# Attention value product with the softmax weights stationary, and v with a column of ones moving

## The chip, the cores and the metric

The program runs on one core of a Trainium2 chip. The metric is the device time of one execution in microseconds (us). Most executions of one kernel agree within 0.3%; lowest and highest are given beside each median. Where two kernels are compared, the ratio is the mean time of one kernel's fast runs over the mean of the other's fast runs of the same rounds on the same chip; it is therefore not quite the ratio of the medians that are quoted beside it.

Engines: PE is TensorE's matmul, PEld its weight load, DVE is VectorE, ACT is ScalarE, POOL is GpSimd, SP is SyncE. The argument takes it that each engine works through its instructions in the program's order, and that only weight loads run ahead.

## The reference, cut to what matters

Block-sparse attention (batch 4, 8 heads, 768 tokens, head dimension 64), then two matmuls that are multiplied, then two more matmuls.

```python
scores = (1 / sqrt(64)) * q @ k^T            # per batch and head
scores = where(mask, scores, -1e9)           # 32x32 blocks; mask is the same for all heads
attn = exp(scores - max) / sum(exp(scores - max))
x = (attn @ v) with heads side by side       # 3072 tokens x 512
out = ((x @ w1) * (x @ w2)) @ w3 @ w_out     # 512 -> 1024 -> 1024 -> 512
```

Both kernels fold `w3 @ w_out` once (the "fold"), and use that as one matrix. Both skip the maximum and multiply the exponentials by a 0/1 mask.

## The kernel before

Work goes in 72 rounds. A round is one (batch b, block of 256 queries t, half of the heads Q, third of the keys kp). Three rounds with kp = 0, 1, 2 make one accumulation. PE's order in a round is: scores of this round, value product of the round before, then two pieces of "filler" (the fold, later the FFN), which run while ACT and DVE turn scores into weights.

```python
def scores(b, t, Q, kp, i):                  # twice a round, i = 0, 1
    ... 4 matmuls into s (PSUM, 2 banks, pool ps_s of two such tiles)
    nc.scalar.activation(e, s, AF.Exp, scale=1.0 / 8.0)
    nc.vector.tensor_tensor(e, e, mask[...], op=ALU.mult)

def values(b, t, Q, kp):
    ...
    for k2 in range(2):
        for part in range(3):                # v columns 0-31, 32-63, then ones
            for g in range(4):               # four heads, one 32-row strip of PSUM each
                rhs = es[i][:, h, k2 * QT:(k2 + 1) * QT]          # 256 queries moving
                ... matmul(d[rows, :], lhsT=ones, rhs=rhs)        # part 2: denominators
                ... matmul(o[rows, ...], lhsT=vn[...32 columns], rhs=rhs)

def normalize(b, t, Q):                      # after kp = 2
    nc.scalar.activation(ln, d, AF.Ln)
    nc.scalar.activation(rec, ln, AF.Exp, scale=-1.0)
    nc.vector.tensor_tensor(X[i][...], o, rec, op=ALU.mult)       # x stands turned already

# FFN filler: ps_f is a pool of two PSUM banks, shared by pa, pb and po
pa: 4 matmuls of 512 columns -> nc.scalar.copy(a, p)
pb: 4 matmuls of 512 columns -> nc.vector.tensor_tensor(hT[:, f, :], p, a, op=ALU.mult)
po: 8 matmuls of 512 columns -> copy -> output DMA

for s, g in enumerate(groups):               # cuts marked ...
    scores(b, t, Q, kp, 0)
    scores(b, t, Q, kp, 1)
    if prev is not None:
        values(*prev)
        finish(prev)                         # normalize if kp == 2
    ...
    pop(0 if s < 3 else 2)                   # two pieces of filler
    prev = g
```

Inputs are loaded and cast by DMAs that GpSimd issues, all in one queue: q, k, v of the first four heads of batch 0, then `w_out` and `w3` with the other four heads in between, then `w1`, `w2`, with later batches behind them.

The softmax here doesn't subtract the row's maximum and nothing guards it: scores larger than these inputs give would overflow.

Of the kernel before, what the change touches and what calls it, by code (L numbers as in the profile page):

```python
# [8 lines left out]
F32 = mybir.dt.float32  # L9
BF16 = mybir.dt.bfloat16  # L10
I32 = mybir.dt.int32
AF = mybir.ActivationFunctionType
ALU = mybir.AluOpType
# [4 lines left out]
def kernel(  # L18
# [16 lines left out]
    nc = tc.nc  # L35
    B, H, S, D = q.shape
    BLK = 32
    NB = S // BLK
    C = S // 128
# [3 lines left out]
    QT = 256  # L43
    NT = S // QT

    def pool(name, bufs, **kw):
        return ctx.enter_context(tc.tile_pool(name=name, bufs=bufs, **kw))

    const = pool("const", 1)
    wts = pool("wts", 1)  # L50
    nat = pool("nat", 4)
    natv = pool("natv", 8)
    qkt = pool("qkt", 8)
    epool = pool("epool", 6)
    small = pool("small", 2)
# [5 lines left out]
    ps_o = pool("ps_o", 1, space=PSUM)  # L61
    ps_f = pool("ps_f", 2, space=PSUM)
# [13 lines left out]
    qn, kn, vn = {}, {}, {}  # L76
# [16 lines left out]
    wf_sb = wts.tile([128, NF, d_model], BF16, tag="wf")  # L93

    def load_w12(ap, t):
        src = ap.rearrange("(Q g s d) f -> g d Q s f", Q=2, g=4, s=2)
        for g in range(4):
            for Q in range(2):
                nc.gpsimd.dma_start(out=t[32 * g:32 * g + 32, 2 * Q:2 * Q + 2, :], in_=src[g][:, Q])


    load_pair(0, 0, "qk")
# [25 lines left out]
    load_pair(0, 3)  # L128
    load_w3(4, NF)
    load_w12(moe_w1, w1_sb)  # L130
    load_w12(moe_w2, w2_sb)

    ident = const.tile([128, 128], BF16, tag="ident")
    nc.vector.tensor_scalar(ident, in0=idf, scalar1=0.0, scalar2=None, op0=ALU.is_equal)
    ones = const.tile([128, 32], BF16, tag="ones")
    nc.vector.memset(ones, 1.0)
    hot = const.tile([NB, C, 128], BF16, tag="hot")
    hot_hi = const.tile([NB, C, 128], BF16, tag="hot_hi")
    nc.vector.tensor_scalar(hot, in0=hotf, scalar1=0.0, scalar2=None, op0=ALU.is_ge)
# [14 lines left out]
    for r in range(3):  # L154
# [3 lines left out]
                                op=ALU.is_equal)  # L158
# [12 lines left out]
    def build_mask(t):  # L171
        for kp in range(3):
            mp = ps_f.tile([128, 512], F32, tag="f", name="mp")
            for k2 in range(2):
                nc.tensor.matmul(mp[:, k2 * QT:(k2 + 1) * QT], lhsT=hot[:, 2 * kp + k2, :],
                                 rhs=G[:, t * QT:(t + 1) * QT], start=True, stop=True)
            nc.scalar.copy(mask[:, t, kp, :], mp)  # L177


    QK = {}  # L180

    def transposes(b, pr):
        tp = ps_s.tile([128, 2, 1024], BF16, tag="s", name="tp")
        for x, src in ((0, qn[b, pr]), (1, kn[b, pr])):
            for c in range(C):
                for h in range(2):
                    nc.tensor.transpose(tp[64 * h:64 * h + 64, x, c * 128:(c + 1) * 128],  # L187
                                        src[:, h, c, :], ident)
        t = qkt.tile([128, 2, S], BF16, tag="qkt", name="qkt")
        nc.vector.tensor_copy(t, tp[:, :, :S])  # L190
        QK[b, pr] = t

    E = {}

# [16 lines left out]
    acc = {}  # L211

    def values(b, t, Q, kp):
        if kp == 0:
            acc["o"] = ps_o.tile([128, 512], F32, tag="o", name="o")
            acc["d"] = ps_o.tile([128, QT], F32, tag="d", name="d")
        o, d = acc["o"], acc["d"]
        es = [E.pop((b, t, Q, kp, i)) for i in range(2)]
        for k2 in range(2):
            kc = 2 * kp + k2  # L220
            first, last = kc == 0, kc == C - 1
            for part in range(3):
                for g in range(4):
                    i, h = divmod(g, 2)
                    rhs = es[i][:, h, k2 * QT:(k2 + 1) * QT]
                    rows = slice(32 * g, 32 * g + 32)
                    if part == 2:
                        nc.tensor.matmul(d[rows, :], lhsT=ones, rhs=rhs, start=first, stop=last,  # L228
                                         skip_group_check=True)
                    else:  # L230
                        nc.tensor.matmul(o[rows, part * QT:(part + 1) * QT],  # L231
                                         lhsT=vn[b, 2 * Q + i][:, h, kc, 32 * part:32 * part + 32],
                                         rhs=rhs, start=first and part == 0, stop=last,
                                         skip_group_check=True)

    X = {}

    def normalize(b, t, Q):
        o, d = acc["o"], acc["d"]
        i, half = divmod(b * NT + t, 2)  # L240
        if i not in X:
            X[i] = xpool.tile([128, 4, 512], BF16, tag="x", name="x")
        ln = small.tile([128, QT], F32, tag="ln", name="ln")
        nc.scalar.activation(ln, d, AF.Ln)  # L244
        rec = small.tile([128, 1, QT], F32, tag="rec", name="rec")
        nc.scalar.activation(rec[:, 0, :], ln, AF.Exp, scale=-1.0)  # L246
        nc.vector.tensor_tensor(  # L247
            X[i][:, 2 * Q:2 * Q + 2, half * QT:(half + 1) * QT],
            o.rearrange("p (s n) -> p s n", s=2),
            rec.to_broadcast((128, 2, QT)), op=ALU.mult)  # L250


    fill = deque()
# [27 lines left out]
    def ffn(i):  # L281
        x = X[i]
        hT = hpool.tile([128, NF, 512], BF16, tag="h", name="h")
        box = {}

        def pa(f):
            def go():
                p = ps_f.tile([128, 512], F32, tag="f", name="pa")
                for c in range(4):
                    nc.tensor.matmul(p, lhsT=w1_sb[:, c, f * 128:(f + 1) * 128], rhs=x[:, c, :],  # L290
                                     start=c == 0, stop=c == 3)
                a = apool.tile([128, 512], BF16, tag="a", name="a")
                nc.scalar.copy(a, p)  # L293
                box["a"] = a
            return go

        def pb(f):
            def go():
                p = ps_f.tile([128, 512], F32, tag="f", name="pb")
                for c in range(4):  # L300
                    nc.tensor.matmul(p, lhsT=w2_sb[:, c, f * 128:(f + 1) * 128], rhs=x[:, c, :],  # L301
                                     start=c == 0, stop=c == 3)
                nc.vector.tensor_tensor(hT[:, f, :], p, box["a"], op=ALU.mult)  # L303
            return go

        def po(n, half):
            def go():
                if half == 0:
                    box["o"] = ps_f.tile([128, 512], F32, tag="f", name="po")
                for f in range(4 * half, 4 * half + 4):  # L310
                    nc.tensor.matmul(box["o"], lhsT=hT[:, f, n * 128:(n + 1) * 128],  # L311
                                     rhs=wf_sb[:, f, :], start=f == 0, stop=f == NF - 1)
                if half == 1:
                    b, c = divmod(4 * i + n, C)
                    ob = opool.tile([128, 512], F32, tag="ob", name="ob")
                    nc.vector.tensor_copy(ob, box["o"])  # L316
                    nc.sync.dma_start(out=outv[b, c], in_=ob)
            return go

        for f in range(NF):  # L320
            fill.append(pa(f))
            fill.append(pb(f))
        for n in range(4):
            fill.append(po(n, 0))
            fill.append(po(n, 1))


    transposes(0, 0)
    transposes(0, 1)
    for t in range(NT):  # L330
        build_mask(t)

# [11 lines left out]
    done = {}  # L344
    n_ffn = 0
    prev = None

    def finish(g):
        nonlocal n_ffn
        b, t, Q, kp = g  # L350
        if kp == 2:
            normalize(b, t, Q)
            done[b * NT + t] = done.get(b * NT + t, 0) + 1
            while done.get(2 * n_ffn) == 2 and done.get(2 * n_ffn + 1) == 2:
                ffn(n_ffn)
                n_ffn += 1

    def pop(n):
        for _ in range(n):
            if fill:  # L360
                fill.popleft()()

    for s, g in enumerate(groups):
        b, t, Q, kp = g
        r = s % 18
        scores(b, t, Q, kp, 0)
        scores(b, t, Q, kp, 1)
        if prev is not None:
            values(*prev)
            finish(prev)  # L370
        if b + 1 < B and r in (2, 5, 8, 11):
            load_pair(b + 1, (r - 2) // 3)
        if b == 0 and s in (7, 8):
            transposes(0, s - 5)
        elif b + 1 < B and r in (12, 13, 15, 16):
            transposes(b + 1, (12, 13, 15, 16).index(r))
        pop(0 if s < 3 else 2)
        prev = g
    values(*prev)
    finish(prev)  # L380
    while fill:
        pop(1)
    order.__exit__(None, None, None)
# [30 lines left out]
```

## Time and profile before

299.68 us, median of 2 runs (299.67 to 299.69).

| what | view | value |
|---|---|---|
| busy share PE / DVE / ACT | the page's first part | 91% / 65% / 63% |
| PE in the chain that ended last | the chain of waits | 68% |
| a round with FFN filler: scores / values / filler | the timeline | 0.54 / 0.77 / 1.83 us |
| three such rounds | the timeline | 9.62 us |
| first value matmul | the timeline | 23.70 us |

The first part of the page of the kernel before. Columns: engine, busy us, share of the span, instructions.

```profile
PE 272.0 (91%) x3412; PEld 141.2 (47%) x3412; DVE 194.2 (65%) x308; ACT 189.5 (63%) x250; POOL 49.6 (17%) x81
```

One round of the kernel before, from the timeline of PE. Columns: start, length to the end of the last matmul, engine, source line, what is written from what, shape, count. Lengths overlap, because matmuls are pipelined; so read costs as differences of starts.

```profile
136.77 0.61 PE L201 MATMUL s<-qkt 64*128 64x256 bf16 x8
137.31 0.40 PE L231 MATMUL o<-e,vn 128*32 128x256 bf16 x8
137.54 0.28 PE L228 MATMUL d<-e,ones 128*32 128x256 bf16 x4
137.65 0.39 PE L231 MATMUL o<-e,vn 128*32 128x256 bf16 x8
137.87 0.28 PE L228 MATMUL d<-e,ones 128*32 128x256 bf16 x4
138.08 1.04 PE L290 MATMUL pa<-x,w_sb 128*128 128x512 bf16 x4
138.96 1.03 PE L301 MATMUL pb<-x,w_sb 128*128 128x512 bf16 x4
139.92 0.28 PE L201 MATMUL s<-qkt 64*128 64x256 bf16 x2
```

Scores take 137.31 - 136.77 = 0.54 us, the value product 138.08 - 137.31 = 0.77, pa and pb 1.84. There is no gap: PE is the limit here. Four value matmuls of 256 columns run side by side on 32-column strips, 0.11 us per four.

In the waits of PE (columns: who waited for whom, us in total, times, longest) in the kernel before:

```profile
PE o L231 <- DVE x L247: 1.8, 2, 1.1
```

The trace has the fold's transposes, eight in a row with a full weight load each.

```profile
48.69 0.62 PE L259 MATMUL w3p<-ident,w_sb 128*128 128x128 bf16 x8
```

One of them lasts 0.22 us, so the other seven started within 0.40 us, 57 ns apart: a 128x128 weight load is hidden behind 128 moving columns.

### The profile page before, as it was taken

The numbers are of one execution on the slowest core, as the hardware profiler recorded it, in microseconds if no ns is written. First come the engines' busy times: TensorE is split into PE (matmuls) and PEld (weight loads), VectorE is DVE, ScalarE is ACT, GpSimd is POOL, SyncE is SP. The second block draws the span as 40 slices with busy tenths as digits, with TensorE's granted clock in tenths as the row PEclk, the third lists the DMA queues.
The fourth block names the chain that finished last, engine by engine and source line by source line (L and its number), as shares of the span: only waits on it lengthen the run. The fifth ranks groups of instructions, "written<-read, shape, count | busy, mean of one in ns | idle before, by whom it ended". The sixth has DMA issues, their size and how long they took to land.

```text
span 298.6 us, 7850 instructions
## 1 busy us (share of the span) xinstructions
PE 272.0 (91%) x3412; PEld 141.2 (47%) x3412; DVE 194.2 (65%) x308; ACT 189.5 (63%) x250; POOL 49.6 (17%) x81
## 2 busy tenths in 40 slices
PE   0479888987999999999999999999999999999994
PEld 0335455555454455555455455555445445444441
DVE  3616787778767776776777677677767676643332
ACT  1088766656688886576867887657988778721310
POOL 8634487222200000332100000000000000000000
PEclk9999999999999999999999999999999999999998
DMA  7999999973420002757311000011000120003003
GB/s 96 150 204 207 206 173 186 180 106 55 66 44 2 0 2 108 131 69 106 55 37 73 35 2 2 2 72 70 3 2 1 52 93 2 0 2 140 0 12 129
DMA packets 20053, 21.46 MB, mean 72 GB/s; under 512 B 1588, under 2 KB 14900, under 8 KB 20020
## 3 DMA queue, kind: packets, MB, share of 16 engines
q0 software_dynamic: 16528, 14.68, 32.5%
q1 hardware_dynamic: 3492, 6.29, 5.6%
q8 instruction: 26, 0.43, 0.6%
q14 instruction: 7, 0.06, 0.1%
HBM read 29.36 MB, written 6.29 MB: 119 GB/s over the span
## 4 chain that ended last, share of the span: by engine, by line
PE 68%; ACT 15%; DVE 10%; issue 4%; POOL 1%; ACTq 0%; POOLq 0%
PE o L231 13%; PE pa L290 12%; PE pb L301 12%; ACT e L206 10%; PE po L311 10%; PE s L201 9%; PE wp L272 5%; DVE x L247 4%; PE d L228 4%; ACT rec L246 3%; PE tp L187 3%; DVE qkt L190 2%; ACT ln L244 2%; DVE e L207 1%; ACT mask L177 1%
## 5 line engine op out<-in xcount | busy, mean ns | idle before, releaser
L206 ACT ACTIVATE e<-s 128x1024 bf16<-128x1024 f32 x144 | 139.5, 1021 | 54.8 <-PE s L201 54.4
L207 DVE TENSOR_TENSOR e<-e,mask 128x1024 bf16<-128x1024 bf16 x144 | 99.1, 691 | 55.3 <-ACT e L206 55.3
L231 PE MATMUL o<-e,vn 128*32 128x256 bf16 x1152 | 54.8, 278 | 3.8 <-DVE x L247 1.8
L201 PE MATMUL s<-qkt 64*128 64x256 bf16 x576 | 47.5, 277 | 5.6 <-DVE qkt L190 3.9
L290 PE MATMUL pa<-x,w_sb 128*128 128x512 bf16 x192 | 49.7, 381 | 0.0
L301 PE MATMUL pb<-x,w_sb 128*128 128x512 bf16 x192 | 49.2, 379 | 0.0
L303 DVE TENSOR_TENSOR h<-pb,a 128x512 bf16<-128x512 f32 x48 | 33.1, 690 | 21.2 <-PE pb L301 21.2
L311 PE MATMUL po<-wf_sb,h 128*128 128x512 bf16 x192 | 44.5, 380 | 0.0
L293 ACT CAST a<-pa 128x512 bf16<-128x512 f32 x48 | 28.0, 583 | 26.1 <-PE pa L290 25.7
L228 PE MATMUL d<-e,ones 128*32 128x256 bf16 x576 | 42.4, 276 | 0.0
L201 PEld LDWEIGHTS <-qkt 64*128 64x128 bf16 x576 | 22.8, 95 | 37.5 <-issue 34.8
L231 PEld LDWEIGHTS <-vn 128*32 128x32 bf16 x1152 | 26.9, 96 | 20.5 <-issue 18.4
L301 PEld LDWEIGHTS <-w_sb 128*128 128x128 bf16 x192 | 18.7, 98 | 24.1 <-issue 2.6
L311 PEld LDWEIGHTS <-h 128*128 128x128 bf16 x192 | 17.5, 98 | 21.9 <-issue 2.7
L290 PEld LDWEIGHTS <-w_sb 128*128 128x128 bf16 x192 | 15.7, 98 | 21.1 <-issue 7.0
L316 DVE COPY ob<-po 128x512 f32<-128x512 f32 x24 | 16.5, 688 | 10.2 <-PE po L311 10.2
L85 POOL DMA_DIRECT2D qn<-in_q_dram x16 | 11.7, 728 | 66.7 <-PE tp L187 59.4
L247 DVE TENSOR_TENSOR x<-o,rec 128x512 bf16<-128x512 f32 x24 | 16.6, 692 | 1.6 <-ACT rec L246 0.9
L228 PEld LDWEIGHTS <-ones 128*32 128x32 bf16 x576 | 17.0, 98 | 0.4
L190 DVE COPY qkt<-tp 128x1536 bf16<-128x1536 bf16 x16 | 15.2, 950 | 1.3 <-PE tp L187 1.3
L272 PE MATMUL wp<-wo_sb,w3t_sb 128*128 128x512 bf16 x64 | 15.2, 380 | 0.0
L85 POOL DMA_DIRECT2D vn<-in_v_dram x16 | 11.6, 726 | 17.5 <-PE d L228 14.6
(54 smaller groups left out, 125.7 us busy)
## 6 DMA issues: line engine op xcount, KB each, us to landing
out_dram<-ob SPq DMA_DIRECT2D x24, 256.0 KB, 2.0
qn<-in_q_dram POOLq DMA_DIRECT2D x16, 192.0 KB, 4.2
kn<-in_k_dram POOLq DMA_DIRECT2D x16, 192.0 KB, 4.8
vn<-in_v_dram POOLq DMA_DIRECT2D x16, 192.0 KB, 5.8
w_sb<-in_moe_w_dram POOLq DMA_DIRECT2D x8, 256.0 KB, 10.6
w_sb<-in_moe_w_dram POOLq DMA_DIRECT2D x16, 128.0 KB, 5.3
wo_sb<-in_moe_w_out_dram POOLq DMA_DIRECT2D x1, 1024.0 KB, 11.3
rand_sb<-in_sampled_blocks_dram SPq DMA_DIRECT2D x1, 0.6 KB
```

Source lines behind the costliest of these rows:

```text
L201: nc.tensor.matmul(s[:, h, k2 * QT:(k2 + 1) * QT], lhsT=qk[64 * h:64 * h + 64, 1, kc * 128:(kc + 1) * 128], rhs=qk[64 * h:64 * h + 64, 0, ...
L206: nc.scalar.activation(e, s, AF.Exp, scale=1.0 / 8.0)
L207: nc.vector.tensor_tensor(e, e, mask[:, t, kp:kp + 1, :].to_broadcast((128, 2, 512)), op=ALU.mult)
L228: nc.tensor.matmul(d[rows, :], lhsT=ones, rhs=rhs, start=first, stop=last, skip_group_check=True)
L231: nc.tensor.matmul(o[rows, part * QT:(part + 1) * QT], lhsT=vn[b, 2 * Q + i][:, h, kc, 32 * part:32 * part + 32], rhs=rhs, start=first and ...
L247: nc.vector.tensor_tensor(X[i][:, 2 * Q:2 * Q + 2, half * QT:(half + 1) * QT], o.rearrange("p (s n) -> p s n", s=2), rec.to_broadcast((128 ...
L272: nc.tensor.matmul(box["p"], lhsT=w3t_sb[:, j, i * 128:(i + 1) * 128], rhs=wo_sb[:, j, :], start=j == 0, stop=j == NF - 1)
L290: nc.tensor.matmul(p, lhsT=w1_sb[:, c, f * 128:(f + 1) * 128], rhs=x[:, c, :], start=c == 0, stop=c == 3)
L293: nc.scalar.copy(a, p)
L301: nc.tensor.matmul(p, lhsT=w2_sb[:, c, f * 128:(f + 1) * 128], rhs=x[:, c, :], start=c == 0, stop=c == 3)
L303: nc.vector.tensor_tensor(hT[:, f, :], p, box["a"], op=ALU.mult)
L311: nc.tensor.matmul(box["o"], lhsT=hT[:, f, n * 128:(n + 1) * 128], rhs=wf_sb[:, f, :], start=f == 0, stop=f == NF - 1)
```

## The change

Its intent: swap the operands of the value product. The weights `e` (128 keys x 128 queries) are loaded, and v with a column of ones (65 columns) moves. One matmul then gives 64 outputs and the denominator; 24 matmuls of 256 columns (four abreast) become 16 of 65 columns. The price is that x comes out with tokens on partitions: it is divided there (ln and exp on ACT disappear), and then turned by four PE transposes with a copy from PSUM. v has to be widened to 65 columns, which GpSimd does.

```diff
-    natv = pool("natv", 8)
+    natv = pool("natv", 4)
+    vpool = pool("vpool", 8)
@@ loads of w1, w2: sixteen DMAs of permuted rows become eight of plain rows (cut)
+    def widen(b, pr):
+        t = vpool.tile([128, 2, C, D + 1], BF16, tag="v1", name="v1")
+        nc.gpsimd.memset(t[:, :, :, D:], 1.0)
+        nc.gpsimd.tensor_copy(t[:, :, :, :D], vn[b, pr])
+        V1[b, pr] = t
@@ values (the tile o grows to two PSUM banks, d and the ones go; cut)
-            for part in range(3):
-                ... (d and o, 32 columns stationary, 256 moving)
+            for i in range(2):
+                for h in range(2):
+                    g = 2 * i + h
+                    for qt in range(2):
+                        lo = k2 * QT + qt * 128
+                        nc.tensor.matmul(o[:, qt, g * (D + 1):(g + 1) * (D + 1)],
+                                         lhsT=es[i][:, h, lo:lo + 128],
+                                         rhs=V1[b, 2 * Q + i][:, h, kc, :],
+                                         start=kc == 0 and g == 0, stop=kc == C - 1, ...)
@@ normalize
-        nc.scalar.activation(ln, d, AF.Ln)
-        nc.scalar.activation(rec[:, 0, :], ln, AF.Exp, scale=-1.0)
-        nc.vector.tensor_tensor(X[i][...], o..., rec..., op=ALU.mult)
+        nc.vector.reciprocal(rec, o[:, :, :, D:])
+        nc.vector.tensor_tensor(xn, o[:, :, :, :D], rec..., op=ALU.mult)
+        def go():
+            tp = ps_f.tile([128, 2, 2, 128], BF16, tag="f", name="xp")
+            for s in range(2):
+                for qt in range(2):
+                    nc.tensor.transpose(tp[:, s, qt, :], xn[:, qt, 2 * s:2 * s + 2, :], ident)
+            nc.vector.tensor_copy(xi[...], tp...)
+            ...
+        turn.append(go)
@@ the loop
         if prev is not None:
             values(*prev)
+            turned()                         # the transposes of the round before
             finish(prev)
@@ before the loop, and with each transposes(...) of q and k
+    widen(0, 0)
+    widen(0, 1)
```

More of the change, by code (lines that the diff above doesn't have):

```diff
@@ L95, in load_w12 @@
     def load_w12(ap, t):
-        src = ap.rearrange("(Q g s d) f -> g d Q s f", Q=2, g=4, s=2)
-        for g in range(4):
-            for Q in range(2):
-                nc.gpsimd.dma_start(out=t[32 * g:32 * g + 32, 2 * Q:2 * Q + 2, :], in_=src[g][:, Q])
+        for c in range(4):
+            nc.gpsimd.dma_start(out=t[:, c, :], in_=ap[128 * c:128 * c + 128, :])
     load_pair(0, 0, "qk")
@@ L134 @@
     nc.vector.tensor_scalar(ident, in0=idf, scalar1=0.0, scalar2=None, op0=ALU.is_equal)
-    ones = const.tile([128, 32], BF16, tag="ones")
-    nc.vector.memset(ones, 1.0)
     hot = const.tile([NB, C, 128], BF16, tag="hot")
@@ L180 @@
     QK = {}
+    V1 = {}
     def transposes(b, pr):
@@ L214, in values @@
         if kp == 0:
-            acc["o"] = ps_o.tile([128, 512], F32, tag="o", name="o")
-            acc["d"] = ps_o.tile([128, QT], F32, tag="d", name="d")
-        o, d = acc["o"], acc["d"]
+            acc["o"] = ps_o.tile([128, 2, 512], F32, tag="o", name="o")
+        o = acc["o"]
         es = [E.pop((b, t, Q, kp, i)) for i in range(2)]
@@ L220, in values @@
             kc = 2 * kp + k2
-            first, last = kc == 0, kc == C - 1
-            for part in range(3):
-                for g in range(4):
-                    i, h = divmod(g, 2)
-                    rhs = es[i][:, h, k2 * QT:(k2 + 1) * QT]
-                    rows = slice(32 * g, 32 * g + 32)
-                    if part == 2:
-                        nc.tensor.matmul(d[rows, :], lhsT=ones, rhs=rhs, start=first, stop=last,
-                                         skip_group_check=True)
-                    else:
-                        nc.tensor.matmul(o[rows, part * QT:(part + 1) * QT],
-                                         lhsT=vn[b, 2 * Q + i][:, h, kc, 32 * part:32 * part + 32],
-                                         rhs=rhs, start=first and part == 0, stop=last,
+            for i in range(2):
[6 more added lines that the diff above has]
+                                         rhs=V1[b, 2 * Q + i][:, h, kc, :],
+                                         start=kc == 0 and g == 0, stop=kc == C - 1,
                                          skip_group_check=True)
     X = {}
+    turn = deque()
     def normalize(b, t, Q):
-        o, d = acc["o"], acc["d"]
+        o = acc["o"][:, :, :4 * (D + 1)].rearrange("p s (g e) -> p s g e", e=D + 1)
         i, half = divmod(b * NT + t, 2)
@@ L242, in normalize @@
             X[i] = xpool.tile([128, 4, 512], BF16, tag="x", name="x")
-        ln = small.tile([128, QT], F32, tag="ln", name="ln")
-        nc.scalar.activation(ln, d, AF.Ln)
-        rec = small.tile([128, 1, QT], F32, tag="rec", name="rec")
-        nc.scalar.activation(rec[:, 0, :], ln, AF.Exp, scale=-1.0)
-        nc.vector.tensor_tensor(
-            X[i][:, 2 * Q:2 * Q + 2, half * QT:(half + 1) * QT],
-            o.rearrange("p (s n) -> p s n", s=2),
-            rec.to_broadcast((128, 2, QT)), op=ALU.mult)
+        xi = X[i]
+        rec = small.tile([128, 2, 4, 1], F32, tag="rec", name="rec")
+        nc.vector.reciprocal(rec, o[:, :, :, D:])
+        xn = small.tile([128, 2, 4, D], BF16, tag="xn", name="xn")
+        nc.vector.tensor_tensor(xn, o[:, :, :, :D], rec.to_broadcast((128, 2, 4, D)), op=ALU.mult)
+        def go():
[3 more added lines that the diff above has]
+                    nc.tensor.transpose(tp[:, s, qt, :], xn[:, qt, 2 * s:2 * s + 2, :], ident)
+            nc.vector.tensor_copy(
+                xi[:, 2 * Q:2 * Q + 2, half * QT:(half + 1) * QT],
+                tp.rearrange("p s t n -> p s (t n)"))
+            done[b * NT + t] = done.get(b * NT + t, 0) + 1
+        turn.append(go)
     fill = deque()
@@ L352, in finish, with turned @@
             normalize(b, t, Q)
-            done[b * NT + t] = done.get(b * NT + t, 0) + 1
-            while done.get(2 * n_ffn) == 2 and done.get(2 * n_ffn + 1) == 2:
-                ffn(n_ffn)
-                n_ffn += 1
+    def turned():
+        nonlocal n_ffn
+        while turn:
+            turn.popleft()()
+        while done.get(2 * n_ffn) == 2 and done.get(2 * n_ffn + 1) == 2:
+            ffn(n_ffn)
+            n_ffn += 1
     def pop(n):
@@ L374 @@
             transposes(0, s - 5)
+            widen(0, s - 5)
         elif b + 1 < B and r in (12, 13, 15, 16):
             transposes(b + 1, (12, 13, 15, 16).index(r))
+            widen(b + 1, (12, 13, 15, 16).index(r))
         pop(0 if s < 3 else 2)
@@ L380 @@
     finish(prev)
+    turned()
     while fill:
```

## The prediction

> **What bounds it now.** TensorE: the page gives PE 91% busy (DVE 65%, ACT 63%), and the chain of waits has PE 68%. The timeline shows the steady round from 80 to 260 us: scores 0.54 us, value product 0.77, eight 512-wide filler matmuls (FFN) 1.83; 3.15 together, three rounds 9.63. The 24 value matmuls run four at a time on 32-column tiles: 0.11 us per four of 256 columns, plus about 0.1 us of empty array at each change of tile shape (the Trainium skill, "TensorEngine Tiling (Array Packing)", Key Properties, says a change of tiling mode drains; the gaps agree).
>
> **What the value product gains.** 24 matmuls of 256 columns, four abreast, become 16 of 65 columns on the whole array, each with a 128-column weight load. The fold's transposes (the timeline: eight in 0.62 us, one 0.22) start 57 ns apart with a 128x128 load each, so loads hide behind 128 columns. Scaled to 65 columns: estimate 30 ns each, 0.48 us per round; no drain before the FFN. The round falls to about 2.85 us, worth 0.3 us in 72 rounds if PE never waited. ACT loses ln and exp (19.4 us busy).
>
> **What is added.** Per (batch, tile, half), every third round: four PE transposes (0.22 us); on DVE a reciprocal (estimate 0.2 us), the same multiply (0.69) and a copy from PSUM (0.42, as the fold's). Three things put PE in new waits:
>
> 1. *Start, +14 us.* v is widened on GpSimd. The instruction order puts the first two widenings behind all weight-load issues. GpSimd's timeline shows that queue throttled: each issue waits for the completion of the eighth before it. The eighth w1/w2 issue came at 34.9 us, so I expect the widenings at 35.5 to 37.5 (about 1 us each, estimated from the 0.82 us iota of 768). The first value product, at 23.7 us before, waits until about 37.7. PE is in order; nothing recovers this.
> 2. *Accumulator.* Scores start at 0; the second mask multiply ends at 3.09; then reciprocal and multiply on in-order DVE free the accumulator at 4.05. The next values would come at 3.39: a wait of 0.66 us per three rounds (0.19 before).
> 3. *PSUM ring.* The transposed tile takes one of the two buffers that pa and pb rotate through, and its copy stands behind both masks on DVE (ends 3.64 us into the round). pb wants that buffer at 2.77: about 0.9 us lost where the round has pa and pb (14 of 18 after the fold).
>
> **Sum.** After the fold (53 rounds): -15.7 from shorter rounds, +12.4 from wait 2 and transposes, +12.7 from wait 3, -4 where q/k transposes fill the waits: about +5. Fold stage about +1. Tail +1 (the last transposes wait for the last multiply). Start +14. Total +21: **320 us**, range 309 to 332. Faster by over 2%: 2%; within 2%: 4%; slower by over 2%: 94%.
>
> **What would show it.** Timeline: first value matmul near 37.7 us, after a PE gap of some 12 us released by the GpSimd copy; value group about 0.5 us; three-round period about 10.3 us in pa/pb stretches, 9.4 in po stretches. Waits: PE pb (or the buffer's next user) on the DVE x copy, some 10 us in total; PE o on the DVE xn multiply, some 10. ACT busy near 170 us; PE busy share below 85%.
>
> **What would make it wrong.** Widening early or much slower; 65-column matmuls held by their weight loads (up to 57 ns each would add 0.4 us per round, about 20 us); contrariwise, if wait 3 hides, about 309.

## The result

323.08 us, median of 2 runs (322.72 to 323.43), against 299.68: ratio 1.078, 95% interval 1.075 to 1.081. Slower, and inside the stated range.

The first part of the page of the changed kernel:

```profile
PE 261.4 (81%) x2932; PEld 141.6 (44%) x2932; DVE 207.5 (65%) x355; ACT 171.2 (53%) x202; POOL 61.1 (19%) x105
```

PE has less to do and is idle more: 91% busy before, 81% now. To find where, I cut the spans of the profiled executions at the starts of the scores of rounds 3, 20 and 72, the same work in both kernels (from the timelines):

| stretch | before, us | changed, us | difference |
|---|---|---|---|
| start, to round 3 | 25.28 | 38.28 | +13.0 |
| fold, rounds 3 to 19 | 56.27 | 56.43 | +0.2 |
| FFN filler, rounds 20 to 71 | 174.67 | 182.78 | +8.1 |
| round 72 and the rest | 42.4 | 43.4 | +1.0 |

**The start.** GpSimd's timeline of the changed kernel (DMA issues, then the widening):

```profile
34.02 0.53 POOL L98 DMA_DIRECT2D w_sb<-in_moe_w_dram  x1 [0.71 <-DMA w_sb<-in_moe_w_dram]
35.28 0.53 POOL L98 DMA_DIRECT2D w_sb<-in_moe_w_dram  x1 [0.74 <-DMA w_sb<-in_moe_w_dram]
35.80 0.17 POOL L194 MEMSET v<- 128x12 bf16 x1
35.84 0.84 POOL L195 COPY v<-vn 128x768 bf16<-128x768 bf16 x1
36.61 0.16 POOL L194 MEMSET v<- 128x12 bf16 x1
36.65 0.83 POOL L195 COPY v<-vn 128x768 bf16<-128x768 bf16 x1
```

PE's timeline of the changed kernel at the same time. The brackets give idle time before the group, and what ended it:

```profile
23.16 0.61 PE L206 MATMUL s<-qkt 64*128 64x256 bf16 x4 [0.30 <-ACT e L211]
36.73 0.38 PE L230 MATMUL o<-v,e 128*128 128x65 bf16 x4 [12.96 <-POOL v L195]
37.53 0.82 PE L230 MATMUL o<-v,e 128*128 128x65 bf16 x12 [0.42 <-POOL v L195]
38.28 1.04 PE L206 MATMUL s<-qkt 64*128 64x256 bf16 x8
```

The widening takes 1.7 us in all; it comes late only because it stands behind the last weight load in GpSimd's queue, and each of those issues waits for an older load to land (the brackets). PE waits 13 us for it.

**The FFN stretch.** A normalizing round and the one after it, from the timeline of the changed kernel (lines of all engines; weight loads left out, other cuts marked ...):

```profile
102.09 0.61 PE L206 MATMUL s<-qkt 64*128 64x256 bf16 x8
...
102.64 0.66 PE L230 MATMUL o<-v,e 128*128 128x65 bf16 x16
103.14 1.02 PE L299 MATMUL pa<-x,w_sb 128*128 128x512 bf16 x4
103.58 0.69 DVE L212 TENSOR_TENSOR e<-e,mask 128x1024 bf16<-128x1024 bf16 x1 [0.62 <-ACT e L211]
...
104.50 0.69 DVE L212 TENSOR_TENSOR e<-e,mask 128x1024 bf16<-128x1024 bf16 x1 [0.22 <-ACT e L211]
104.96 0.61 PE L206 MATMUL s<-qkt 64*128 64x256 bf16 x8
105.11 0.20 DVE L246 RECIPROCAL rec<-o 128x8 f32<-128x8 f32 x1
105.34 0.69 DVE L248 TENSOR_TENSOR xn<-o,rec 128x512 bf16<-128x512 f32 x1
...
106.09 0.67 PE L230 MATMUL o<-v,e 128*128 128x65 bf16 x16 [0.52 <-DVE xn L248]
...
106.59 0.39 PE L254 MATMUL xp<-ident,xn 128*128 128x128 bf16 x4
106.82 1.03 PE L299 MATMUL pa<-x,w_sb 128*128 128x512 bf16 x4
107.88 0.58 ACT L302 CAST a<-pa 128x512 bf16<-128x512 f32 x1 [0.55 <-PE pa L299]
107.97 0.42 DVE L255 COPY x<-xp 128x512 bf16<-128x512 bf16 x1
108.52 1.02 PE L310 MATMUL pb<-x,w_sb 128*128 128x512 bf16 x4 [0.67 <-ACT a L302]
109.47 0.39 PE L206 MATMUL s<-qkt 64*128 64x256 bf16 x4
```

The value product does what was hoped: 16 matmuls in 103.14 - 102.64 = 0.50 us, 31 ns each, and an undisturbed round lasts 104.96 - 102.09 = 2.87 us (3.15 before). But the accumulator is read by the multiply of the normalization, which stands behind both masks on DVE (at 103.58 and 104.50), so the next value product waits 0.52 us. Then pb waits 0.67 us. That round lasts 4.51 us. Three such rounds take 10.25 us against 9.62 before. In the stretches of the output matmul (po), where no pb waits, three rounds take 9.42.

The waits of PE, changed kernel:

```profile
PE o L230 <- POOL v L195: 13.4, 2, 13.0
PE o L230 <- DVE xn L248: 11.1, 16, 1.9
...
PE pb L310 <- ACT a L302: 7.6, 11, 0.7
```

These three waits are 32.1 us in sum, more than the 22 us by which the profiled span grew; the shorter rounds gave the rest back.

One cause I had not foreseen shows only in durations. Mask multiplies were 694 ns at most before. In the changed kernel ten of 144 take over 750 ns, up to 2001 ns, 5.6 us more than ten ordinary ones in sum, and every one of the ten overlaps a widening copy on GpSimd. Here two of them, from the timelines of DVE and of GpSimd of the changed kernel (two multiplies in a row take 1.28 us when undisturbed):

```profile
62.22 2.30 DVE L212 TENSOR_TENSOR e<-e,mask 128x1024 bf16<-128x1024 bf16 x2 [0.69 <-ACT e L211]
```

```profile
61.92 0.82 POOL L195 COPY v<-vn 128x768 bf16<-128x768 bf16 x1
...
62.73 1.24 POOL L195 COPY v<-vn 128x768 bf16<-128x768 bf16 x1
```

The Trainium skill, "SBUF — State Buffer", section "Who interferes with whom", says that a DVE instruction with two SBUF inputs contends with a GpSimd instruction that reads SBUF, and that the later one is blocked until the first is done. The trace agrees in kind: the mask multiply reads `e` and `mask` from SBUF, the copy reads v, and they lengthen each other here (the two multiplies took 1.07 and 1.30 us in place of 0.69, the second copy 1.24 in place of 0.83).

### The profile page after: what moved, and what is told of

Read it like the earlier page. It is cut to its first block, busy times and chain, and to the rows that moved or that the text cites. A ratio compares the mean times of both kernels' runs of the same rounds, so it can differ in the third digit from the quotient of the medians.

```text
span 320.9 us, 6905 instructions
## 1 busy us (share of the span) xinstructions
PE 261.4 (81%) x2932; PEld 141.6 (44%) x2932; DVE 207.5 (65%) x355; ACT 171.2 (53%) x202; POOL 61.1 (19%) x105
## 4 chain that ended last, share of the span: by engine, by line
PE 54%; DVE 14%; ACT 11%; issue 8%; DMA 7%; POOL 4%; ACTq 0%; POOLq 0%
PE pb L310 11%; PE pa L299 11%; ACT e L211 9%; PE po L320 9%; PE o L230 8%; DMA w_sb<-in_moe_w_dram 7%; DVE e L212 7%; PE s L206 7%; DVE xn L248 4%; PE wp L281 4%; PE tp L186 2%; ACT a L302 2%; DVE qkt L189 2%; PE xp L254 2%; DVE rec L246 1%
## 5 line engine op out<-in xcount | busy, mean ns | idle before, releaser
L212 DVE TENSOR_TENSOR e<-e,mask 128x1024 bf16<-128x1024 bf16 x144 | 104.1, 729 | 60.9 <-ACT e L211 59.2
L230 PE MATMUL o<-v,e 128*128 128x65 bf16 x1152 | 49.6, 196 | 25.3 <-POOL v L195 13.4
L230 PEld LDWEIGHTS <-e 128*128 128x128 bf16 x1152 | 40.3, 99 | 42.7 <-issue 25.3
L299 PEld LDWEIGHTS <-w_sb 128*128 128x128 bf16 x192 | 16.4, 98 | 14.2
L248 DVE TENSOR_TENSOR xn<-o,rec 128x512 bf16<-128x512 f32 x24 | 16.6, 691 | 0.8
L195 POOL COPY v<-vn 128x768 bf16<-128x768 bf16 x16 | 15.5, 980 | 3.1 <-DMA vn<-in_v_dram 3.0
L174 ACT CAST mask<-mp 128x512 bf16<-128x512 f32 x9 | 4.9, 587 | 14.3 <-PE mp L172 14.3
L86 POOL DMA_DIRECT2D kn<-in_k_dram x16 | 11.7, 730 | 3.4 <-PE w3p L268 1.7
```

What stands on the lines that cost most here:

```text
L86: nc.gpsimd.dma_start(out=t, in_=src[b][:, 2 * pr:2 * pr + 2])
L212: nc.vector.tensor_tensor(e, e, mask[:, t, kp:kp + 1, :].to_broadcast((128, 2, 512)), op=ALU.mult)
L230: nc.tensor.matmul(o[:, qt, g * (D + 1):(g + 1) * (D + 1)], lhsT=es[i][:, h, lo:lo + 128], rhs=V1[b, 2 * Q + i][:, h, kc, :], start=kc == ...
L248: nc.vector.tensor_tensor(xn, o[:, :, :, :D], rec.to_broadcast((128, 2, 4, D)), op=ALU.mult)
L299: nc.tensor.matmul(p, lhsT=w1_sb[:, c, f * 128:(f + 1) * 128], rhs=x[:, c, :], start=c == 0, stop=c == 3)
```

## The experiments

Theory: the value product itself became faster, and the time went to (1) the place of two small copies in GpSimd's queue, (2) the accumulator wait, because the normalization stands behind the masks on DVE, (3) the wait of pb, because the transposed tile takes a bank of the filler's pair, and (4), found after the result, GpSimd copies that slow mask multiplies. Rivals: the start was held by loads anyway; the new matmuls or transposes are slow on PE; the order of DVE alone is what matters, and the old kernel could have it too. Ten kernels were run. Each ratio is to the kernel before, of the same rounds; the changed kernel's is 1.078. Stretches and waits are those of the one profiled execution of each kernel.

### e1_early: widen earlier

```diff
     load_w3(2, 4)
+    widen(0, 0)                              # and the two calls before the loop go
+    widen(0, 1)
     load_pair(0, 3)
```

> The changed kernel (323.1 us) with the first two widenings of v moved in GpSimd's order to just behind the fourth w3 load, where GpSimd sat idle from 12.8 to 18.5 us before. Theory (the start stall is only the place of these two copies in GpSimd's queue): first value matmul back near 23.7 us, about 13 us saved, 310 us (309 to 312); three-round period in the pa/pb stretches unchanged at 10.25. Rival (PE would have been held in this stretch anyway, by arrival of weights or of q and k): less than 6 us saved, 317 or more.

Measured: 308.32 us (308.26 to 308.46), ratio 1.0267, a little below my range. The first value matmul starts at 22.92 us in place of 36.73, and the FFN stretch is unchanged (182.80 us). So the stall was the queue's order: some 13 to 14 us (0.8 us of the difference is that the first scores start at 19.74 in place of 20.53 us here, which varies between executions: a profile of the old value product, e7_before_loads, has 19.90) for two copies of 0.84 us that could run from 12.8 us on, where GpSimd only waited, until 18.5 us in the kernel before.

### e2_act: widen on ScalarE

```diff
-        nc.gpsimd.memset(t[:, :, :, D:], 1.0)
-        nc.gpsimd.tensor_copy(t[:, :, :, :D], vn[b, pr])
+        nc.vector.memset(t[:, :, :, D:], 1.0)
+        nc.scalar.copy(t[:, :, :, :D], vn[b, pr])
```

> The changed kernel with all sixteen widenings moved from GpSimd to ScalarE (the ones column to VectorE). Start theory: the stall of 13 us goes, so 310 or less. Contention theory (the GpSimd copies slow the mask multiplies that run beside them; ten multiplies took 1.0 to 2.0 us in place of 0.69): all 144 mask multiplies back at 0.69 us, and 1 to 3 us below the run with early widening, 307 to 309. If those slow multiplies cost nothing, it equals the early widening, 310.

Measured: 306.31 us (305.09 to 307.59), ratio 1.0213 (1.0168 to 1.0259), 2.0 us below e1_early, whose interval (1.0252 to 1.0282) it just touches. Against the kernel before, 2% is inside this interval. Two of the four runs are near 305.1 and two near 307.6 us, for no cause that the record shows, and the profiled one is of the former; so this run alone does not settle contention. All 144 mask multiplies are at 694 ns or less. The FFN stretch is 180.81 us, 2.0 less than in e1_early, and the fold 1.4 less.

### e3_last: masks behind the normalization

```diff
-        nc.vector.tensor_tensor(e, e, mask[...], op=ALU.mult)      # in scores()
 ...
             turned()
             finish(prev)
+        masks(*g)                            # the same two multiplies
```

> The changed kernel with one thing changed: on VectorE the two mask multiplies of a round stand behind the normalization and the copy of the transposed tile, not in front. Same work. Theory (8 us lost between 95 and 277 us, and the gain of the shorter round, went to waits on VectorE order: the accumulator, and the filler's second buffer): three-round period 10.25 falls to about 8.8, 18 to 24 us saved, 298 to 305 us; start stall of 13 us unchanged. Rival (the 65-column product or the transposes are themselves slow on PE): period stays above 9.6, 315 or more.

Measured: 304.78 us (304.03 to 306.88), ratio 1.0159 (1.0117 to 1.0202). Three rounds take 8.82 us, in pa/pb and in po stretches alike, and the FFN stretch falls from 182.78 to 163.73 us. The start stall is still there (first value matmul at 36.20 us). This settles the rival: nothing on PE is slow; with the same instructions in another order, the FFN stretch is 11 us faster than in the kernel before. The fold took 58.71 us in the profiled run, 2.3 more than in the changed kernel: there the clock row of the page (40 slices of 7.6 us) shows a lower clock from about 15 to 53 us, before, in and behind the stall,

```profile
PEclk9975577999999999999999999999999999999998
```

and one round of the fold took 7.40 us (4.44 in the changed kernel). That round also holds a wait of 2.31 us for a slowed mask multiply; I did not separate the two. The profile of e9_norm_first has the same 7.40 us round, again with both.

### e8_early_last: both

The edits of e1_early and e3_last together.

> Both: early widening and masks last. If the two losses are independent they add: 323 - 13 - 18 to 24 = 286 to 292 us, faster than the kernel before (299.7) by 3 to 4 per cent. If PE then meets another limit (ScalarE at 2.6 us of work per round, or the score-exp-mask chain), 293 to 299.

Measured: 288.76 us (288.63 to 289.13), ratio 0.9617 (0.9602 to 0.9632): faster than the kernel before by 3.8%. In units of the ratio the two edits alone gave 0.051 and 0.062, which is 0.113, and together 0.116: they add. A normalizing round and the next, from the timeline of this kernel (PE and DVE lines):

```profile
202.41 0.61 PE L208 MATMUL s<-qkt 64*128 64x256 bf16 x8
...
203.65 0.21 DVE L252 RECIPROCAL rec<-o 128x8 f32<-128x8 f32 x1 [0.38 <-PE o L236]
203.90 0.69 DVE L254 TENSOR_TENSOR xn<-o,rec 128x512 bf16<-128x512 f32 x1
...
204.50 1.28 DVE L219 TENSOR_TENSOR e<-e,mask 128x1024 bf16<-128x1024 bf16 x2
...
205.82 0.67 PE L236 MATMUL o<-v,e 128*128 128x65 bf16 x16
206.32 0.39 PE L260 MATMUL xp<-ident,xn 128*128 128x128 bf16 x4
206.55 1.03 PE L305 MATMUL pa<-x,w_sb 128*128 128x512 bf16 x3
206.75 0.42 DVE L261 COPY x<-xp 128x512 bf16<-128x512 bf16 x1 [0.36 <-PE xp L260]
...
207.41 1.03 PE L316 MATMUL pb<-x,w_sb 128*128 128x512 bf16 x4
```

DVE now waits for PE at the reciprocal, the accumulator is free long before 205.82, and the copy of the turned tile comes 0.43 us after the transposes begin. No bracket stands on a PE line.

### e6_xp_s: the transposed tile in the scores' buffers

```diff
-            tp = ps_f.tile([128, 2, 2, 128], BF16, tag="f", name="xp")
+            tp = ps_s.tile([128, 4, 512], BF16, tag="s", name="xp")[:, 0:1, :]...
```

> The changed kernel with the transposed tile in the scores' pair of PSUM buffers instead of the filler's pair. Theory: this takes away only the third wait (pb held while pa's buffer is evacuated, 7.6 us in 11 waits in the trace), the accumulator wait stays: three-round period in pa/pb stretches 10.25 falls to about 9.45, total 314 to 317. Rival (pb waits for something else on ScalarE that stays): no change, 322 to 324.

Measured: 316.22 us (315.02 to 317.47), ratio 1.0523, a gain of 0.026 on the changed kernel. pa/pb triples take 9.41 to 9.42 us in place of 10.25; the wait of pb is gone from the list (not shown), and the accumulator wait stays:

```profile
PE o L230 <- DVE xn L248: 10.7, 16, 1.9
```

The FFN stretch is 175.49 us: taking wait 3 away was worth 7.3 us there. That is net of a new cost: the q/k transposes use the scores' buffers too, and now wait 4.6 us in 12 waits in place of 1.5 in 5 (1.7 us of the increase lies in the FFN stretch).

### e9_norm_first: only the normalization ahead of the masks

```diff
         if prev is not None:
             values(*prev)
+            if kp == 0:
+                finish(prev)
+        masks(*g)                            # masks() as in e3_last
+        if kp:
             turned()
-            finish(prev)
```

> The changed kernel with only the normalization (reciprocal and multiply) ahead of the masks on VectorE; the copy of the transposed tile stays behind them. Theory: takes away only the accumulator wait (PE o on the xn multiply, 11 us); pb still waits in the round with the transposes, now about 0.9 us because it comes sooner: period about 9.7 in pa/pb stretches and 8.8 in po stretches, total 311 to 315. Rival (the accumulator wait hides behind others): 320 or more.

Measured: 314.93 us (313.60 to 316.25), ratio 1.0479. Triples take 9.66 to 9.71 us with pa and pb and 8.82 with po. The wait on the xn multiply is gone; that of pb is not:

```profile
PE pb L314 <- ACT a L306: 7.6, 11, 0.7
```

The FFN stretch is 173.68 us: taking wait 2 away was worth 9.1 us there (summed from the timeline, 7.4 are the value product's wait, and 1.7 a wait of the scores for the copy of q and k on DVE, which shrank with it). With the 7.3 of wait 3 that is 16.4 of the 19.1 us that e3_last took away by both. Of the missing 2.7 us, 1.7 can be the new waits that e6_xp_s brought; the rest I did not pull apart.

### e4_act_last: widening on ScalarE, masks last

The edits of e2_act and e3_last together.

> Widening on ScalarE and masks last on VectorE. If contention between GpSimd copies and mask multiplies matters also without the order waits, 1 to 3 us below early widening with masks last; if ScalarE (53 per cent busy, 13 us more here) becomes the limit in the rounds with q/k transposes, equal to it or slower by up to 3 us.

Measured: 286.15 us (285.75 to 286.55), ratio 0.9522 (0.9502 to 0.9542): the fastest of all, 4.8% below the kernel before, and below e8_early_last (0.9617) clear of both intervals. All mask multiplies are at 694 ns or less again, and ACT, with 182.7 us busy in a span of 284.7, holds PE little (the first line below). PE's longest waits besides the 10.6 us at the very start (which the kernel before has too):

```profile
PE s L206 <- ACT e L211: 4.2, 8, 1.1
PE s L206 <- DVE v L194: 1.7, 2, 0.9
```

Its FFN stretch is 162.35 us, 12.3 below the kernel before and 1.4 below e8_early_last; its fold is 1.8 us below that of e8_early_last. In the FFN stretch the difference can be located: three groups of three rounds are longer in e8_early_last, by 0.5, 0.4 and 0.5 us, and they follow the three multiplies that are slowed there (at 79.16, 126.09 and 137.62 us, each 1.27 us long beside a GpSimd copy). The other fourteen groups agree within 0.01 us.

### e5_before_last: the kernel before with masks last

The edit of e3_last on the kernel before.

> The kernel before (299.7 us) with its two mask multiplies behind the normalization on VectorE. Rival to be tested: the gain of masks last is a matter of order that the old value product could have had as well (then 292 to 297 us). Theory: not so, since its normalization waits for ln and exp on ScalarE, which stand behind both score exponentials; the multiply cannot start before 3.1 us of the round, the masks end at 5.2, and the next values wait over a microsecond each third round: 312 to 322 us, slower.

Measured: 325.89 us (325.17 to 326.04), ratio 1.0837, slower and a little beyond my range. Three rounds take 10.82 us in place of 9.62; in its waits the value product is held by the masks:

```profile
PE o L235 <- DVE e L212: 17.7, 32, 1.7
```

So the order that helps the changed kernel harms the old one. The old normalization needs ACT, where ln and exp stand behind the score exponentials, and the masks then stand behind it; the new one needs only the value product and DVE. The fold grew too, which I had not counted.

### e7_before_loads: only the loads of the change

The kernel before with the changed loads of w1 and w2. The result is wrong (rows of the weights no longer match x).

> The kernel before with only the change's w1 and w2 loads (eight of 256 KB with plain rows, in place of sixteen). Its result is wrong on purpose: the rows of w1 and w2 then don't stand as the old x does. Theory: these loads carry no part of the difference, 299 to 301 us. Rival (the other order or shape of the loads holds PE): more than 2 us of change either way.

Measured: 300.32 us (299.56 to 300.90), ratio 1.0006 (0.9973 to 1.0039). The loads carry nothing.

### e10_twice: each widening copy done twice

The kernel e8_early_last, with

```diff
         nc.gpsimd.tensor_copy(t[:, :, :, :D], vn[b, pr])
+        nc.gpsimd.tensor_copy(t[:, :, :, :D], vn[b, pr])
```

> Early widening and masks last (288.8 us), with each widening copy on GpSimd done twice. Contention theory: about twice as many slowed mask multiplies (excess over 0.69 us some 8 to 10 us in sum in place of 4.8), and 1 to 4 us longer, 290 to 293. If the difference of 2.6 us to the version with widening on ScalarE came from something else, the slowed multiplies may double but the time stays within 0.5 us of 288.8.

Measured: 295.33 us (291.97 to 296.54, one of five runs slow), ratio 0.9861 (0.9826 to 0.9895) against 0.9617 for single copies. Slower, as contention says, but sizes miss: slowed multiplies add up to 6.1 us over 0.69 each in the profiled run (4.8 with single copies, 8 to 10 expected), and the time grew by more than the 1 to 4 us that I expected. The profiled run was the fastest of the five, 3.1 us above the profiled run of e8_early_last. Of these, 0.8 us is a later start of the scores (20.52 in place of 19.74 us), which is not the copies' doing as far as is known, 0.4 lies in the fold and 1.9 in the FFN stretch. There two waits of PE grew: that of the value product for a mask multiply from 0.6 to 1.9 us, and that of the scores for the copy of q and k on DVE from 0.4 to 1.0. PE's waits name no load, so a later issue of loads behind the doubled copies is not what held it. Why the other runs are longer still, the trace does not tell. The sign is shown, the size is not explained.

Copies are not the whole of it either. One of the seven slowed multiplies of e8_early_last (at 57.77 us, 1.31 us long) and two of the eleven here (at 62.76 and 129.11 us) start beside DMA issues of GpSimd, with no widening copy running. In the kernel before, 34 of the 144 multiplies overlap such issues and none is over 694 ns; so what slowed these three stays open.

## Why the prediction was right

Predicted 320 us, measured 323.08. The three places of loss were named rightly, one of them with the wrong releaser; point by point:

- **Value product, "estimate 30 ns each, 0.48 us per round".** Measured 31 ns and 0.50 us; the undisturbed round is 2.87 us where I said about 2.85. The estimate came from the fold's transposes in the trace of before. It also said that no drain stands between values and FFN: pa follows directly at 103.14.
- **Start, "+14 us", widenings at 35.5 to 37.5, first value product at about 37.7.** Measured +13.0; widenings from 35.80 to 37.48; first value matmul at 36.73. It started a little sooner than I said, as the first four matmuls need only the first copy. e1_early shows the cause.
- **Accumulator, "a wait of 0.66 us per three rounds", "some 10" us.** 0.52 us in an undisturbed triple, 11.1 us in sum with some longer ones. The reciprocal took 0.20 us and the multiply 0.69. e9_norm_first takes this wait away alone.
- **PSUM ring, "pb wants that buffer", "its copy stands behind both masks on DVE", "about 0.9 us".** The wait is there and the cure (e6_xp_s) works, but I named the wrong releaser. The built program's memory plan puts xp in one bank and both pa and pb of that round in the other (in 11 rounds, as many as there are waits), so pb waits until ACT has evacuated pa (0.67 us, 7.6 us in 11 waits), not for the copy of xp (no wait of pb on it in the trace). I had assumed strict rotation through the two banks. The term was 12.7 us in my sum and 7.6 in the trace.
- **"-4 where q/k transposes fill the waits".** Mis-sized. A normalizing round with q/k transposes takes the same in both kernels (scores from 116.71 to 120.84 before, from 132.00 to 136.14 changed: 4.13 and 4.14 us). So such rounds kept none of the 0.3 us, as PE now also waits there for a score buffer (five waits of about 0.3 us on ACT).
- **Not in the sum: contention of GpSimd copies with mask multiplies**, about 2 us in the FFN stretch (e1_early against e2_act). Together: FFN stretch "about +5", measured +8.1; the over-sized ring wait and these under-sized terms partly cancelled. So the nearness of the two totals is in part luck.
- **Fold "about +1", tail "+1", PE busy below 85%, ACT near 170 us, triples of 10.3 and 9.4 us.** Measured +0.2, +1.0, 81%, 171.2, 10.25 and 9.42.

What the prediction did not say is that the loss was avoidable. With e4_act_last the FFN stretch is 12.3 us shorter than before, which the changed value product makes possible; as written, the change placed its new small operations where in-order queues made PE wait 32 us for them.

## What to carry to other kernels

When a change puts a new small operation into an in-order queue, ask what stands in front of it there, not what it costs: here copies of 0.84 us cost 13 us, and a reciprocal and a multiply of 0.9 us cost 7 to 9. If the limiting engine gets faster, retime the work behind it: of the two orders of masks and normalization tried on both, the one that was better for the old value product was worse for the new one, and the other way round. And try to keep GpSimd's reads of SBUF away from DVE operations with two SBUF inputs that are on the critical path: with masks last, moving the copies off GpSimd was worth 2.6 us here.

## What the Trainium skill lacked or had wrong

- "TensorEngine Tiling (Array Packing)", Key Properties, says that a change of tiling mode drains the array, without a size. From the starts in the trace of before it is about 0.1 us: pb starts at 138.96, streams four times 512 columns in about 0.86 us (as pa does in the changed kernel, from 103.14 to the start of pb at 104.00), and the scores start at 139.92.
- "TensorE: Matmul & The Clock Gate", section "Back-to-back issue gap", gives about 81 ns per matmul of 128 columns as the sustained rate with a weight load each. Here such pairs started 57 ns apart (w3p), and pairs with 65 columns 31 ns apart over 16 in a row.
- "SBUF — State Buffer", section "Who interferes with whom", describes the contention that e2_act takes away, without a cost for this pair: a mask multiply of 0.69 us took 1.0 to 2.0 us beside GpSimd copies of 0.83 us.
- "TensorE: Matmul & The Clock Gate", Part 1, warns that trace events of the throttle can be unreliable; nothing is wrong there, and the runs agree. Eight score matmuls took 1.04 us early in the changed kernel (at 20.53 us, before the 13 us stall, and at 38.28, after it; 0.61 later), though its profile gives a full clock throughout; the kernel before, without the stall, shows the same 1.04 us at 20.52 and 25.28. So no run here shows that the stall lowered the clock.
